# Batch 0 loaded in runs of nine rows, cast on chip and transposed in bf16; other loads released later; instruction order from a priority table that counts tile switches

## The chip, the cores and the metric

The kernel runs on one core of a Trainium2 chip. A core has five engines that each work through a queue of their own in order: TensorE (PE, matrix products and transposes into the eight PSUM banks), VectorE (DVE), ScalarE (ACT), GpSimd (POOL) and SyncE (SP, which here only issues transfers). Sixteen DMA engines move data for all queues. Engines and transfers wait for each other on semaphores. The metric is the device time of one execution in microseconds.

## The reference

Linear attention with exponential features, then a gated unit with a causal convolution of five taps. Eight batches, eight heads, 576 rows, head width 64, 128 features, model width 512.

```python
def phi(x):                                   # x: q or k
    proj = np.einsum('bhsd,df->bhsf', x, w_phi)
    proj = proj - np.max(np.abs(proj), axis=-1, keepdims=True)
    return np.concatenate([np.exp(proj), np.exp(-proj)], axis=-1)
q_p, k_p = (phi(q), phi(k))
kv = np.einsum('bhsf,bhsd->bhfd', k_p, v)
z = np.sum(k_p, axis=2)
num = np.einsum('bhsf,bhfd->bhsd', q_p, kv)
den = np.einsum('bhsf,bhf->bhs', q_p, z)[..., None] + 1e-06
attn = num / den                              # heads side by side give x: (batch, 576, 512)
gate_pre[:, s] = sum over k of conv_w[k] * x[:, s - 4 + k]      # zero before the first row
out = ((1 / (1 + np.exp(-gate_pre))) * (x @ w_val)) @ w_out
```

## The kernel before

A planner in the kernel's source builds the program. `build` makes a list of operations; each has a name, the engine or engines that may run it, an estimated duration, what it reads and writes, a priority (`prio`, smaller is earlier) and for some an earliest time (`rel`). `Plan.schedule` plays them through a list scheduler: at each moment a free engine takes, of the operations whose inputs are there, whose PSUM banks are free and whose `rel` has passed, the one with the smallest priority. The planner's times are used for nothing but the order; `Plan.emit` writes the instructions to the engines' queues in that order, with the semaphore waits that the data needs. So `rel` is not a wait on the chip: a later `rel` only puts a transfer further back in its queue.

A batch goes through these operations (in brackets the number per batch):

- loads. q and k of batches 1 to 7: `cast` [4] is a GpSimd transfer from f32 to bf16 into a DRAM buffer R, `tr` [4] a transposing SyncE transfer of R into KT or QT. v comes by `v` [2] and `vt` [1, four transfers]. Two halves, g = 0 and 1, hold four heads each.
- batch 0 has another way, since nothing can be prefetched for it: `xf` [4, SyncE, lines 417 to 422] loads q and k in f32 as 18 blocks of 128x128 each, 512 contiguous bytes at a time, in the order k g=0, q g=0, k g=1, q g=1, into XF, which lies in the space of batch 1's QTIL (shown as QTIL in the profile); `T0` [12, three transposes each, line 428] turns them on TensorE in f32, and `T0c` [12] copies PSUM to KT or QT.
- features of k: `K`, `Kt` project on TensorE; `Kmax` takes the row maxima on VectorE; `Kexp` the exponentials of both signs on ScalarE, without subtracting the maxima; `MN` and `EK` make exp of the maxima; `VT`, `VTt` (GpSimd, line 537 and 547) scale v by it.
- features of q: `QA`, `Qmax`, `MQ`, `MQc` find the maxima and turn them; `QF` projects and subtracts them, `Qexp` exponentiates.
- `KV` [2] and its copy `KVc`; `NUM` [4] and `NUMt` with `RCP` and `NRM` (division); `XT`, `XTt`, `XTc` transpose the result.
- `GATE` [4] is the convolution as products with diagonal matrices DG (built once by GpSimd, line 397), `TANH` the gate, `VAL` [4] the value product, `GV` their product; `OUT` [4, in odd batches 5], `OUTc`, `store`.

Operations of different products use different shapes of TensorE's array: 128*128 (KV, NUM, XT, MQ, OUT), 64*128 (K, QA, QF, VAL), 128*64 (GATE, NUMt, XTt), and 64*32 or 128*32 for small rests.

The priority of an operation is `period * batch + offset`, with one offset per name and one step (`Kd`, `QAd` and so on) per index; `limit` says how many PSUM tiles of a kind may live at once. Weights (`WVa`, `WO`) are loaded by GpSimd with casts at priorities -195 and -194, w_phi and conv_w by ScalarE's queue.

Of the kernel before, what the change touches and what calls it, by code (L numbers as in the profile page):

```python
# [8 lines left out]
AF = mybir.ActivationFunctionType  # L9
# [21 lines left out]
PE_L = 0.19  # L31
# [8 lines left out]
    off=dict(  # L40
        cast=-28.24, v=-6.0, DG=8.07, K=0.0, Kd=4.34, QA=1.0, QAd=4.0, EK=2.83, VT=1.85, MQ=15.13,
        QF=19.55, QFd=3.59, KV=21.26, KVd=3.55, NUM=27.88, NUMd=3.0, XT=1.6, GATE=41.98, GATEd=3.0,
        OUT=55.38, OUTd=1.94, store=0.5,
# [21 lines left out]
class Plan:  # L65
# [4 lines left out]
    def __init__(self):  # L70
        self.ops, self.tok = [], {}
# [6 lines left out]
    def op(self, name, eng, occ, fn, prio, r=(), w=(), ps=None, new=False, vis=None, dma=None, key=None,  # L78
           rel=0.0):
# [8 lines left out]
        o.name, o.fn, o.prio, o.dma, o.key, o.ps, o.new, o.rel = name, fn, prio, dma, key, ps, new, rel  # L88
        hard, soft = set(), set()
# [19 lines left out]
        o.deps = [(x, True) for x in hard] + [(x, False) for x in soft]  # L109
# [7 lines left out]
    def _from(self, x, hard, e):  # L117

        if x.eng == e:
            return x.t2 if hard and e != "PE" else x.t1  # L120
        return x.t2 + WAKE

    def schedule(self, limit):
# [8 lines left out]
        for o in self.ops:  # L132
            if not o.need:
                for e in o.opts:
                    ready[e].append(o)
# [6 lines left out]
        order = []  # L142
        left = len(self.ops)
        while left:
# [4 lines left out]

            while pend and pend[0][0] <= t + 1e-9:  # L150
                s, _, o = heapq.heappop(pend)
                dma_now = self._share(queues, dma_now, s, times)
                queues.setdefault(o.eng, []).append([o, o.dma])
            dma_now = self._share(queues, dma_now, t, times)
# [4 lines left out]
            while again:  # L159
                again = False  # L160
                for e in self.ENG:
# [25 lines left out]
                    for f in o.opts:  # L187
                        ready[f].remove(o)
                    o.eng, o.t0 = e, t
                    o.t1, o.t2 = t + o.occ[e], t + o.vis[e]  # L190
                    if o.dma is not None:
                        o.t2 = 1e9
                        heapq.heappush(pend, (o.t1 + 0.6, o.seq, o))
                        heapq.heappush(times, o.t1 + 0.6)
# [3 lines left out]
                    if ps is not None:  # L198
# [8 lines left out]
                        else:  # L207
# [3 lines left out]
                            if not ps.left:  # L211
# [4 lines left out]
                                heapq.heappush(times, o.t2 + WAKE)  # L216
                    for x in (o.t1, o.t2, o.t2 + WAKE):
                        if x < 1e8:
                            heapq.heappush(times, x)
                    order.append(o)  # L220
                    for c in o.outs:
                        c.need -= 1
                        if not c.need:
                            for f in c.opts:
                                ready[f].append(c)
        self.order = order
        for s, _, o in pend:
            queues.setdefault(o.eng, []).append([o, o.dma])
        self._share(queues, dma_now, 1e7, times)
# [3 lines left out]
    def _share(queues, now, t, times):  # L233
        import heapq
        while now < t:
# [9 lines left out]
            for y in act:  # L245
                y[0][1] -= d / len(act)
                if y[0][1] < 1e-9:
                    o = y.pop(0)[0]
                    o.t2 = now + 1.4
                    heapq.heappush(times, o.t2)  # L250
                    heapq.heappush(times, o.t2 + WAKE)
# [12 lines left out]
    def emit(self, tc, nc):  # L264
# [29 lines left out]
        with tc.tile_critical(name="main"):  # L294
            for o in self.order:
# [10 lines left out]
                for k, n in need.items():  # L306
                    E.wait_ge(sems[k], n)
                    for kk, nn in snap[(k, n)].items():
                        if kn.get(kk, 0) < nn:
                            kn[kk] = nn  # L310
                out = o.fn(E, None if o.ps is None else o.ps.at)
# [20 lines left out]
def build(pl, cfg, nc=None, m=None):  # L332
# [13 lines left out]
    def const(name, eng, occ, fn, prio, r=(), w=(), **kw):  # L346
# [13 lines left out]
          -150, r=["ident_f"], w=["ident_bf"])  # L360
# [32 lines left out]
    const("cwt", "PE", 1.2, cwt, -90, r=["cwb", "idp"], ps=cwps, new=True)  # L393
    const("CWT", "DVE", 0.15, lambda E, b: [E.tensor_copy(m.CWT[:, :], m.PS[:, b, 0:48])], -89, w=["CWT"], ps=cwps)
    pl.fresh("DG")
    for h in range(H):
# [5 lines left out]
        m.WV[0:D, :, :], m.w_val.rearrange("(h c) j -> c h j", c=D))], -195, w=["WVa"], dma=3.1, key=("WVa",))  # L402
# [547 lines left out]
```

## Time and profile before

| | us |
|---|---|
| median of 2 runs | 258.6 (258.54 to 258.65) |
| the profiled execution | 258.6 |
| its span, first to last instruction | 256.8 |
| TensorE busy | 206.9 |
| VectorE busy | 181.5 |
| ScalarE busy | 174.6 |
| GpSimd busy | 119.1 |

The page of the profile gives busy time per engine, the chain of waits that ended last, groups of instructions by line, and the DMA queues. Views of the trace add the instructions in order of time, waits, and busy time by stretch. L428 is line 428 of the kernel's source. A row of the time line merges neighbouring instructions of one group; its last brackets give the idle time of the engine before them and what ended it.

### The profile page before, as it was taken

How to read it: one execution, taken by the hardware profiler on the slowest of the kernel's cores; microseconds unless marked ns; L12 is line 12 of the kernel's file. 1: busy time of each engine (PE TensorE's matmuls, PEld its weight loads, DVE VectorE, ACT ScalarE, POOL GpSimd, SP SyncE). 2: the span in 40 equal slices, each digit the busy share in tenths (PEclk: the TensorE clock that was granted, in tenths of full speed). 3: DMA queues.
4: the chain of work that ended last, by engine and by line, in shares of the span. 5: the costliest groups of instructions: out<-in, count | busy, mean ns of one | idle time of the engine just before them, and what ended most of it. 6: DMA issues, size and time to landing. Idle time of an engine off the chain costs nothing.

```text
span 256.8 us, 8459 instructions
## 1 busy us (share of the span) xinstructions
PE 206.9 (81%) x3693; PEld 144.7 (56%) x3708; DVE 181.5 (71%) x277; ACT 174.6 (68%) x240; POOL 119.1 (46%) x203
## 2 busy tenths in 40 slices
PE   0260838487968999899899999998998999999960
PEld 0250626466646577657675766576666766775520
DVE  0163583696679977997899778997898797376450
ACT  5031468963498899788898978878998895662300
POOL 8434396477418575716863572167316904200000
PEclk9999977897999999999999999999999999999997
DMA  6999999999535999789999993960170013103041
GB/s 185 200 242 213 315 235 198 240 214 240 131 67 67 214 232 304 150 96 193 214 227 214 250 211 97 218 187 19 21 211 31 3 52 136 24 0 151 17 162 43
DMA packets 58495, 39.95 MB, mean 156 GB/s; under 512 B 39381, under 2 KB 53333, under 8 KB 57946
## 3 DMA queue, kind: packets, MB, share of 16 engines
q1 hardware_dynamic: 56336, 30.03, 49.3%
q0 software_dynamic: 1952, 9.31, 20.2%
q8 instruction: 29, 0.48, 0.8%
q10 hardware_dynamic: 170, 0.08, 0.1%
q14 instruction: 8, 0.07, 0.1%
HBM read 30.48 MB, written 17.69 MB: 188 GB/s over the span
## 4 chain that ended last, share of the span: by engine, by line
PE 59%; DVE 16%; ACT 11%; DMA 9%; issue 2%; SPq 0%; DVEq 0%
PE PS L787 11%; PE PS L813 10%; DMA QTIL<-in_k_dram 9%; PE PS L776 9%; PE PS L665 7%; ACT QTIL L625 6%; DVE MQb L586 5%; PE PS L701 4%; ACT KTIL L500 3%; DVE MK L495 3%; PE PS L612 3%; PE PS L720 2%; PE PS L490 2%; PE PS L618 2%; DVE GV L792 2%
## 5 line engine op out<-in xcount | busy, mean ns | idle before, releaser
L537 POOL TENSOR_TENSOR VT<-VN,EK 128x512 bf16<-128x512 f32 x64 | 65.7, 1045 | 18.8 <-ACT EK L528 18.7
L625 ACT ACTIVATE QTIL<-PS 128x1024 bf16<-128x1024 f32 x64 | 61.9, 1036 | 12.6 <-PE PS L618 12.6
L500 ACT ACTIVATE KTIL<-PS 128x1024 bf16<-128x1024 f32 x64 | 62.5, 1032 | 6.4 <-PE PS L490 4.3
L586 DVE TENSOR_REDUCE MQb<-PS 128x8 bf16<-128x1024 f32 (+1 forms) x40 | 44.1, 1113 | 3.1 <-PE PS L574 2.6
L495 DVE TENSOR_REDUCE MK<-PS 128x8 f32<-128x1024 f32 x32 | 39.0, 1219 | 4.6 <-PE PS L490 2.7
L792 DVE SCALAR_TENSOR_TENSOR GV<-GS,PS 128x576 bf16<-128x576 bf16 x32 | 24.1, 753 | 18.8 <-PE PS L787 14.6
L787 PE MATMUL PS<-XT,WV 64*128 64x288 bf16 x512 | 37.1, 283 | 0.1
L782 ACT ACTIVATE GS<-PS 128x576 bf16<-128x576 f32 x32 | 21.1, 661 | 19.6 <-PE PS L776 19.3
L525 POOL TENSOR_SCALAR MK<-MK 128x16 f32<-128x16 f32 (+1 forms) x24 | 5.9, 244 | 58.6 <-DVE MK L495 55.3
L776 PE MATMUL PS<-XT,DG 128*64 128x288 bf16 x384 | 30.1, 292 | 2.4 <-ACT QTIL L625 1.4
L813 PE MATMUL PS<-WO,GV 128*128 128x512 bf16 x113 | 28.3, 379 | 2.9 <-DVE GV L792 1.1
L787 PEld LDWEIGHTS PS<-XT,WV 64*128 64x128 bf16 x512 | 22.9, 94 | 8.8 <-issue 1.6
L665 PE MATMUL PS<-VT,KTIL 128*128 128x65 bf16 x512 | 22.6, 202 | 2.2 <-ACT QTIL L625 1.3
L776 PEld LDWEIGHTS PS<-XT,DG 128*64 128x64 bf16 x384 | 19.2, 110 | 8.4 <-ACT QTIL L625 1.7
L665 PEld LDWEIGHTS PS<-VT,KTIL 128*128 128x128 bf16 x512 | 20.2, 103 | 5.1 <-issue 4.3
L715 DVE TENSOR_TENSOR XN<-PS,RC 128x512 bf16<-128x512 f32 x32 | 22.0, 690 | 0.9
L701 PE MATMUL PS<-KVSB,QTIL 128*128 128x65 bf16 x512 | 20.6, 193 | 1.3 <-DVE MQb L586 0.9
L547 POOL TENSOR_TENSOR VTt<-VNt,EK 128x512 bf16<-128x512 f32 x16 | 16.6, 1042 | 9.3 <-ACT EK L528 9.2
L428 PE MATMUL PS<-ident_f,QTIL 128*128 128x128 f32 x36 | 8.7, 425 | 14.2 <-DMA QTIL<-in_k_dram 12.7
L701 PEld LDWEIGHTS PS<-KVSB,QTIL 128*128 128x128 bf16 x512 | 17.4, 97 | 4.3 <-DVE MQb L586 1.4
L679 DVE CAST KVSB<-PS 128x520 bf16<-128x520 f32 x16 | 11.2, 699 | 11.5 <-PE PS L670 11.3
L813 PEld LDWEIGHTS PS<-WO,GV 128*128 128x128 bf16 x128 | 11.1, 98 | 12.0 <-DVE GV L792 1.2
(74 smaller groups left out, 285.2 us busy)
## 6 DMA issues: line engine op xcount, KB each, us to landing
VN<-in_v_dram SPq DMA_DIRECT2D x16, 512.0 KB, 6.2
out_dram<-OS SPq DMA_DIRECT2D x32, 256.0 KB, 3.4
R<-in_k_dram POOLq DMA_DIRECT2D x14, 288.0 KB, 6.1
R<-in_q_dram POOLq DMA_DIRECT2D x14, 288.0 KB, 6.3
QTIL<-in_k_dram SPq DMA_DIRECT2D x2, 576.0 KB, 14.6
QTIL<-in_q_dram SPq DMA_DIRECT2D x2, 576.0 KB, 19.6
VNt<-in_v_dram SPq DMA_DIRECT2D x32, 32.0 KB, 4.4
out_dram<-OS SPq DMA_DIRECT2D x16, 64.0 KB, 2.0
```

The lines of the kernel that those rows point to most:

```text
L495: pl.op("Kmax", "DVE", dve(1024), lambda E, at, u=u: [E.tensor_reduce(MK[:, 0, 8 * u:8 * u + 8].rearrange("p (t x) -> p t x", t=2), m.PS[: ...
L500: pl.op("Kexp", "ACT", act(1024), lambda E, at, u=u, g=g: [E.activation(KTIL[:, g, u, :, :, :], m.PS[:, at:at + 2, :].rearrange("p t (x f) ...
L537: pl.op("VT", "POOL", pool(512), lambda E, at, u=u, hh=hh, a=a, g=g, EK=EK: [E.tensor_tensor(m.VT[s][:, g, u, :, :, 0:D], m.VN[s][:, 4 * h ...
L586: pl.op("Qmax", "DVE", dve(256 * nx), lambda E, at, u=u, nx=nx: [E.tensor_reduce(MQb[:, :].rearrange("p (t s) -> p t s", t=2)[:, :, 4 * u: ...
L625: pl.op("Qexp", "ACT", act(1024), lambda E, at, u=u, g=g: [E.activation(m.QTIL[s][:, g, u, :, :, :], m.PS[:, at:at + 2, :].rearrange("p t ...
L665: res.append(E.matmul(m.PS[:, at + sg, x * E1:(x + 1) * E1], m.KTIL[s][:, sg, 2 * g + a, par, x, :], m.VT[s][:, sg, 2 * g + a, par, x, :], ...
L701: return [E.matmul(m.PS[:, at + g, x * E1:(x + 1) * E1], m.QTIL[s][:, sg, 2 * j + g, par, x, :], m.KVSB[s][:, g, sg, x, :], start=(sg == 0 ...
L715: pl.op("NRM", "DVE", dve(512), lambda E, at, view=view, RC=RC, XN=XN, par=par: [E.tensor_tensor(XN[:, :, par, :].rearrange("p (g x) d -> ...
L776: return [E.matmul(m.PS[ROWS[hh], at + p, 0:HALF], m.DG[:, 2 * jt + hh, 3 * p + dl, :], XT[:, 2 * jt + hh, dl:dl + HALF], start=(dl == 0), ...
L787: return [E.matmul(m.PS[:, at + p, 0:HALF], m.WV[ROWS[p], h, P * jt:P * jt + P], XT[ROWS[p], h, PAD:PAD + HALF], start=(h == 0), stop=(h = ...
L792: pl.op("GV", "DVE", dve(576), lambda E, at, jt=jt, GS=GS: [E.scalar_tensor_tensor(out=m.GV[jt][:, s, :, :], in0=GS[:, :, :], scalar=1.0, ...
L813: return [E.matmul(m.PS[:, at, :], m.GV[jt][:, s, p, P * j:P * j + P], m.WO[:, jt, :], start=(jt == 0), stop=(jt == 3)) for jt in range(4)]
```

## The change

It has five parts.

1. Batch 0's `xf` reads nine rows of 128 as one run of 4608 bytes per partition. A new operation `XB` [12] casts three blocks from f32 to bf16 into a buffer in the space of batch 1's KTIL, on VectorE, ScalarE or GpSimd; `T0` transposes bf16; `T0c` writes each ninth column. Odd batches' `Kexp` wait for all XB and T0, as `Qexp` did for T0.
2. `rel` of other loads: batch 1's casts, v, the weights and later batches' casts get entries in tables `rel1` (batches 0 and 1, absolute) and `rel` (later batches, added to `period * batch`). Batch 1's casts have the entries -30.91, 14.39, -96.98 and -10.45, negative ones meaning 0; `v` of batches 0 and 1 has 18.34 and 20.69, WVa 26.92, WO 45.71.
3. `weigh` replaces each priority by one from tables for all batches (`fine`) or for batch 0, batch 1 and the last (`first`, `second`, `last`), one entry per name and index, between about -440 and 172. The tables have about 700 entries, left out below but for some lines.
4. The planner counts a change of TensorE's tile shape as 0.095 us, prefers an operation of the present shape by a `bonus` of 4.41, has new durations, releases what waits for a transfer only when it has landed, and limits other numbers of PSUM tiles. `period` is 24.15.
5. Reuse of a buffer on one engine becomes a dependence of the kind that is waited for; RC has four buffers in place of three.

```diff
 CFG = dict(
-    period=19.0,
+    period=24.15,
+    bonus=4.41,
     limit=dict(
-        K=1, QA=1, QF=3, KV=1, NUM=2, XT=2, MQ=1, GATE=1, VAL=1, OUT=2, T0=3,
+        T0=2, K=2, QA=1, MQ=2, QF=4, KV=3, NUM=3, XT=2, GATE=2, VAL=4, OUT=4,
     ),
...
+    fine=dict(
+        v=(24.2, 51.69,), vt=(84.37,), cast=(-13.35, 37.02, -0.83, 14.17,), tr=(-75.29, -368.41, 15.75,
+        -126.26,), K=(-14.91, -0.84, 15.06, 22.29,), Kmax=(-290.23, 59.46, 70.03, 124.55, -17.49,), Kexp=(63.16,
...
+    first=dict(
...
+        WVb=(-41.19,), WO=(11.86,), xf=(65.3, -63.63, -269.39, 65.64,), XB=(89.84, 39.94, 102.51, -55.53, 28.87,
...
+    rel=dict(
+        v=(2.53, 1.56,), vt=(-7.25,), cast=(-16.04, -20.18, -7.87, -25.82,),
+    ),
+    rel1=dict(
+        WVa=(26.92,), WO=(45.71,), v=(18.34, 20.69,), vt=(17.22,), cast=(-30.91, 14.39, -96.98, -10.45,),
     ),
...
-        o.deps = [(x, True) for x in hard] + [(x, False) for x in soft]
+        o.deps = [(x, True) for x in hard] + [(x, True) for x in soft]
...
+    def weigh(self, cfg):
+        T, last = cfg["period"], max(o.b for o in self.ops)
+        for o in self.ops:
+            for part, on in (("fine", True), ("first", o.b == 0), ("second", o.b == 1), ("last", o.b == last)):
+                x = cfg.get(part, {}).get(o.name)
+                if on and x is not None and o.idx < len(x):
+                    o.prio = T * o.b + x[o.idx]
+            x = cfg.get("rel" if o.b > 1 else "rel1", {}).get(o.name)
+            if x is not None:
+                o.rel = max(0.0, T * o.b * (o.b > 1) + x[o.idx])
...
+                        now = (o.prio - bonus if o.mode is not None and o.mode == pe_mode else o.prio, o.seq)
+                        if best is not None and now >= best_now:
                             continue
...
+                    if e == "PE":
+                        sw = PE_SWITCH if pe_mode is not None and o.mode != pe_mode else 0.0
+                        pe_mode = o.mode
...
-                    src = (m.k, m.q)[xi][0].rearrange("h s d -> (h s d)").rearrange("(c p x) -> p c x", p=P, x=P)
+                    src = (m.k, m.q)[xi][0].rearrange("h s d -> (h s d)").rearrange("(g p cx) -> g p cx", g=2, cx=9 * P)
                     pl.fresh(("XF", xi, g))
                     pl.op("xf", "SP", 0.6, lambda E, b_, xi=xi, g=g, src=src: [E.dma_start(
-                        m.XF[:, 18 * xi + 9 * g:18 * xi + 9 * g + 9, :], src[:, 9 * g:9 * g + 9, :])],
-                        -300 + 2 * g + xi, w=[("XF", xi, g)], dma=1.95, key=("XF", xi, g))
+                        m.XF[:, 18 * xi + 9 * g:18 * xi + 9 * g + 9, :].rearrange("p c x -> p (c x)"), src[g])],
+                        -300 + 2 * g + xi, w=[("XF", xi, g)], dma=1.5, key=("XF", xi, g))
...
+                        pl.op("XB", ("DVE", "ACT", "POOL"), {"DVE": dve(384, True), "ACT": act(384), "POOL": 0.8},
+                              lambda E, at, c=c: [cp(E, m.XB[:, c:c + 3, :], m.XF[:, c:c + 3, :])],
+                              pr, r=[("XF", xi, g)], w=[("XB", c)])
+                        pl.op("T0", "PE", 0.2, lambda E, at, c=c: [E.transpose(
+                            m.PS[:, at, :].bitcast(BF16)[:, P * y:P * y + P], m.XB[:, c + y, :], m.ident_bf[:, :])
+                            for y in range(3)], pr, r=[("XB", c), "ident_bf"], w=[], ps=ps, new=True, mode="F")
+                        dst = 1152 * g
                         pl.op("T0c", ("DVE", "ACT"), {"DVE": dve(384), "ACT": act(384)},
+                              lambda E, at, X=X, dst=dst, j=j: [cp(
+                                  E, m.T[X][0][:, dst:dst + 1152].rearrange("p (i c) -> p c i", c=9)[:, 3 * j:3 * j + 3, :],
+                                  m.PS[:, at, :].bitcast(BF16)[:, 0:384].rearrange("p (c i) -> p c i", c=3))],
+                              pr, w=[(X, 0, g)], ps=ps)
...
-        if x.name == "T0":
+        if x.name in ("T0", "XB"):
             pl.tok["xfdone"].w.append(x)
```

## Rows read from the trace of the kernel before

**Rows 1.** By stretch: us, busy us (count) per engine, PEclk, DMA share, GB/s
```profile
0.00:26.00 26.00, 7.10 (x74) 5.58 (x74) 7.47 (x19) 6.75 (x6) 12.90 (x30) 1.00 0.97 212
...
26.00:60.00 34.00, 22.40 (x383) 17.40 (x384) 22.75 (x33) 24.56 (x34) 21.99 (x35) 0.84 1.14 236
...
80.00:230.00 150.00, 142.85 (x2708) 99.24 (x2714) 124.88 (x187) 125.59 (x176) 74.92 (x123) 1.00 0.66 144
...
230.00:250.00 20.00, 17.40 (x211) 9.85 (x208) 11.94 (x21) 4.23 (x7) 0.00 (x0) 1.00 0.27 99
```

**Rows 2.** Page, parts 1 and 4: busy per engine; last-ending chain by engine
```profile
PE 206.9 (81%) x3693; PEld 144.7 (56%) x3708; DVE 181.5 (71%) x277; ACT 174.6 (68%) x240; POOL 119.1 (46%) x203
...
PE 59%; DVE 16%; ACT 11%; DMA 9%; issue 2%; SPq 0%; DVEq 0%
```

**Rows 3.** Time line, start: start us, us, engine, line, operation, count [idle before]
```profile
14.16 0.60 PE L490 MATMUL PS<-W,KT 64*128 64x128 bf16 x8 [0.29 <-DVE KT L471]
...
26.35 2.18 PE L428 MATMUL PS<-ident_f,QTIL 128*128 128x128 f32 x9 [6.59 <-DMA QTIL<-in_k_dram]
...
32.70 4.05 POOL L537 TENSOR_TENSOR VT<-VN,EK 128x512 bf16<-128x512 f32 x4
...
37.40 0.29 PE L592 MATMUL PS<-ident_bf,MQb 128*128 128x128 bf16 x1 [2.46 <-DVE MQb L586]
...
49.29 0.93 PE L665 MATMUL PS<-VT,KTIL 128*128 128x65 bf16 x14 [1.30 <-ACT QTIL L625]
...
52.44 1.68 PE L701 MATMUL PS<-KVSB,QTIL 128*128 128x65 bf16 x48 [0.25 <-DVE KVSB L679]
```

**Rows 4.** Time line: KV of batches 0 and 7; last cast; batch 7's K
```profile
40.68 1.06 PE L665 MATMUL PS<-VT,KTIL 128*128 128x65 bf16 x16
...
147.58 0.54 POOL L441 DMA_DIRECT2D R<-in_q_dram  x1
...
193.90 0.39 PE L490 MATMUL PS<-W,KT 64*128 64x128 bf16 x8
...
215.67 0.66 PE L665 MATMUL PS<-VT,KTIL 128*128 128x65 bf16 x16
```

**Rows 5.** Time line of TensorE: first and last row counted, prices between
```profile
93.52 1.16 PE L787 MATMUL PS<-XT,WV 64*128 64x288 bf16 x16
...
94.52 0.39 PE L490 MATMUL PS<-W,KT 64*128 64x128 bf16 x8
...
95.69 1.16 PE L787 MATMUL PS<-XT,WV 64*128 64x288 bf16 x16
...
96.79 0.66 PE L665 MATMUL PS<-VT,KTIL 128*128 128x65 bf16 x16
...
228.70 0.62 PE L720 MATMUL PS<-ident_bf,XN 128*128 128x128 bf16 x8
```

**Rows 6.** DMA queues (packets, MB, share); issues (count, KB, us to landing)
```profile
q1 hardware_dynamic: 56336, 30.03, 49.3%
...
q0 software_dynamic: 1952, 9.31, 20.2%
...
R<-in_k_dram POOLq DMA_DIRECT2D x14, 288.0 KB, 6.1
...
KT<-R SPq DMA_TRANSPOSE x14, 5.5
```

**Rows 7.** Groups by line: busy us, mean ns of one, idle before
```profile
L537 POOL TENSOR_TENSOR VT<-VN,EK 128x512 bf16<-128x512 f32 x64 | 65.7, 1045 | 18.8 <-ACT EK L528 18.7
...
L397 POOL TENSOR_TENSOR DG<-I,CWT 128x384 bf16<-128x384 bf16 x8 | 6.4, 826 | 5.3 <-DVE CWT L394 5.3
...
L378 DVE CAST cwb<-cw 5x512 bf16<-5x512 f32 x1 | 0.4, 414 | 1.1 <-DMA cw<-in_moe_conv_w_dram 1.1
...
L471 DVE CAST KT<-PS 128x384 bf16<-128x384 f32 x5 | 2.6, 544 | 6.7 <-PE PS L428 6.6
```

**Rows 8.** By stretch, as the first group: the granted clock fell
```profile
36.00:42.00 6.00, 4.28 (x54) 3.09 (x55) 2.70 (x4) 3.84 (x7) 3.71 (x5) 0.50 1.13 306
```

More of the change, by code (lines that the diff above doesn't have):

```diff
@@ new lines @@
+    second=dict(
+        v=(40.44, 28.51,), vt=(27.96,), cast=(23.57, 57.22, -17.6, -23.17,), tr=(26.1, 27.48, 90.23, 93.93,),
+        K=(111.65, -3.03, -8.73, 28.89,), Kmax=(-193.96, -26.15, 52.35, 40.92, 13.5,), Kexp=(24.94, -9.91,
+        78.31, 38.75, 57.7, 13.17, -45.9, -26.59, -2.37, 121.42,), MN=(49.47, 93.47, 68.19,), EK=(-89, 13.35,
+        25.02,), VT=(-141.28, -6.07, 37.62, 87.24, 63.36, 32.85, 99.98, 8.89,), VT1=(-251.15, -184.04, 66.09,
+        -76.63,), Kt=(-123.51,), VTt=(-85.09, -111.26,), VTt1=(8.2, -121.3,), QA=(-43.93, 62.57, 31.99, 66.56,
+        -0.8,), Qmax=(-62.38, -23.47, -284.75, 44.06, 76.21,), MQ=(-7.08,), MQc=(65.08,), QF=(59.37, -118.11,
+        73.54, -291.73, 46.87,), Qexp=(-323.62, 58.9, 2.24, -247.94, -150.63, -245.14, 88.11, 150.09, -156.45,
+        35.28,), KV=(15.2, -161.51,), KVc=(-275.02, 1.95,), NUM=(43.93, 48.62, -23.08, 47.59,), RCP=(74.67,
+        -22.86, 95.06, -26.26, 92.85,), NRM=(96.75, 101.65, -0.72, -59.55, -59.48,), XT=(21.52, -116.87,),
+        XTc=(29.22, 47.53, -72.51,), NUMt=(39.47,), XTt=(-55.08,), GATE=(-61.84, -83.13, -33.12, 8.5,),
+        TANH=(-126.15, -3.02, -98.9, -58.71,), VAL=(-204.48, -178.47, 54.38, 12.11,), GV=(-35.77, 140.24, -4.28,
+        9.4,), OUT=(-2.86, 114.61, 87.26, 7.53, 97.4,), OUTc=(-54.65, 21.77, 45.52, 73.45, -23.79,),
+        store=(37.14, 65.94, -14.51, 2.1, 26.12,),
+    ),
@@ new lines @@
+    last=dict(
+        v=(-24.49, 46.58,), vt=(90.74,), cast=(87.65, -4.14, 8.43, -21.92,), tr=(-8.64, -80.95, -5.15, 49.71,),
+        K=(-74.63, -0.22, 51.58, 34.63,), Kmax=(28.59, -59.55, 26.12, 64.06, 62.22,), Kexp=(96.47, -88.6, -9.32,
+        39.15, 17.09, 133.15, -24.24, -124.82, -169.42, 22.3,), MN=(65.13, -72.09, -129.79,), EK=(-15.84, 30.04,
+        -12.95,), VT=(-293.34, 35.47, 33.35, -1.49, -16.59, 49.03, 51.42, -5.56,), VT1=(-18.61, -177.51, 3.26,
+        -249.55,), Kt=(-18.89,), VTt=(66.53, -15.46,), VTt1=(72.62, 66.75,), QA=(11.57, -302.19, 41.84, 29.36,
+        -88.87,), Qmax=(-20.97, 85.06, -272.67, 112.38, 3.18,), MQ=(79.77,), MQc=(45.37,), QF=(66.77, -216.05,
+        -128.06, 24.96, 88.2,), Qexp=(-17.76, -37.99, -182.84, 32.84, 48.45, 20.3, 59.36, -78.56, 55.03,
+        24.22,), KV=(2.99, 69.5,), KVc=(-213.37, 0.89,), NUM=(-244.09, -4.19, 20.32, -395.47,), RCP=(2.89,
+        -63.1, 59.65, 7.73, 110.39,), NRM=(105.64, -31.27, -121.24, -287.88, -0.35,), XT=(64, 25.84,), XTc=(24,
+        -227.02, -307.05,), NUMt=(41.99,), XTt=(-22.29,), GATE=(-105.74, -55.15, 25.2, 13.25,), TANH=(30.13,
+        71.69, -270.96, -86.04,), VAL=(21.67, 34.12, 36.1, 53.01,), GV=(-21.26, 14.5, -27, 4.51,), OUT=(38.35,
+        -148.99, 59.91, 27.95, -299.84,), OUTc=(22.03, -27.67, -47.05, -42.72, -36.29,), store=(-275.16, 50.47,
+        -91.16, 68.38, 8.16,),
+    ),
@@ L141, in schedule, with arm, landed @@
         times = sorted({0.0} | {o.rel for o in self.ops})
-        order = []
+        order, pe_mode = [], None
         left = len(self.ops)
+        def arm(o):
+            o.rdy = {}
+            for e in o.opts:
+                o.rdy[e] = max([o.rel] + [self._from(x, h, e) for x, h in o.deps])
+                ready[e].append(o)
+        def landed(done):
+            for x in done:
+                heapq.heappush(times, x.t2 + WAKE)
+                for c in x.outs:
+                    c.need -= 1
+                    if not c.need:
+                        arm(c)
+        for o in self.ops:
+            if not o.need:
+                arm(o)
         while left:
@@ L215, in schedule @@
                                     bank_free[k] = o.t2 + WAKE
[L216 to L219, printed above, removed]
                     order.append(o)
+                    heapq.heappush(times, o.t1)
+                    if o.dma is not None:
+                        o.t2 = 1e9
+                        heapq.heappush(pend, (o.t1 + 0.6, o.seq, o))
+                        heapq.heappush(times, o.t1 + 0.6)
+                        continue
+                    heapq.heappush(times, o.t2)
+                    heapq.heappush(times, o.t2 + WAKE)
                     for c in o.outs:
@@ L246, in _share @@
                 y[0][1] -= d / len(act)
+            for y in act:
                 if y[0][1] < 1e-9:
@@ L249, in _share @@
                     o.t2 = now + 1.4
-                    heapq.heappush(times, o.t2)
-                    heapq.heappush(times, o.t2 + WAKE)
+                    done.append(o)
         return t
@@ L651, in kv @@
     def kv(b):
+        pl.b = b
         s = b % 2
@@ L906 @@
     m.XN = [t(f"XN{s}", [P, H, 2, D]) for s in range(3)]
-    m.RC = [t(f"RC{s}", [P, 2, 4], FP32) for s in range(3)]
+    m.RC = [t(f"RC{s}", [P, 2, 4], FP32) for s in range(4)]
     m.XNt, m.RCt = [t(f"XNt{s}", [P, 4, D]) for s in two], [t(f"RCt{s}", [P, 4], FP32) for s in two]
```

194 lines of the change are left out of this document (114 added, 80 removed).

## Prediction, made before the change was run

> **What bounds the kernel now.** I read the stages first [rows 1]: per stretch, the busy time of each engine and the DMA share. In the first 26 us TensorE works 7.10 us, VectorE 7.47, ScalarE 6.75, while the sixteen DMA engines are full (0.97): the start is bound by transfers. From 80 to 230 us TensorE is busy 142.85 of 150 us, with VectorE (124.88) and ScalarE (125.59) not far behind; the DMA share is 0.66. At the end TensorE runs almost alone (17.40 of 20 us against 11.94 and 4.23). The chain of waits that ended last agrees: TensorE 59%, VectorE 16%, ScalarE 11%, DMA 9% [rows 2].
>
> The time line of the start shows where this hurts [rows 3]. Third in line, `xf` of k for g=1 lets TensorE begin its transposes at 26.35 us, after 6.59 us of waiting. VT of batch 0 begins on GpSimd at 32.70, the second KV (heads of g=1) on TensorE at 49.29, the first NUM at 52.44.
>
> The steady pace: batch 0's first KV is at 40.68, batch 7's at 215.67, so 175.0/7 = 25.0 us a batch [rows 4]. In the list of TensorE's instructions from 93.52 to 228.70 us (first and last row in [rows 5]), 5.4 batches, I counted 140 places where neighbouring rows change the shape of the array's tile (128*128, 64*128, 128*64, and so on), 26 a batch, and 5.1 us of idle time, 0.9 a batch. One change costs 0.10 us: VAL takes 1.00 us up to the K behind it (same shape, 93.52 to 94.52) and 1.10 up to a KV (other shape, 95.69 to 96.79) [rows 5]. So a batch is 26 x 0.10 = 2.6 of changes, 0.9 idle and, by subtraction, 21.5 of work that no order of instructions removes.
>
> **The change part by part.** The sum is made against the profiled execution: span 256.8 and 1.8 around it, 258.6, which is also the median of the runs.
>
> *The start.* Before the third `xf` landed, the 25.2 us of DMA time (0.97 x 26, [rows 1]) held four `xf`, eight casts (batches 1 and 2) and WV and WO. The software queue took 20.2% of 256.8 = 51.9 us for 9.31 MB [rows 6], 5.6 us a MB: 1.64 us for a cast (0.295 MB), 2.9 for a weight (0.52 MB). Eight casts 13.1 and two weights 5.8 leave 6.3 for the `xf`, 1.6 each. The tables release three casts of batch 1 at 0 and put batch 2's and both weights later, so the four `xf` share with 4.9 us of casts: 6.3 + 4.9 = 11.2, plus 1 before the first issue and something to landing: all four by about 14 us. Batch 0's inputs gain 12 to 16 us. The longer runs may make `xf` cheaper too; I count nothing for it.
>
> What is late next is `v`, which stands on SyncE behind transposes that wait for the casts. Up to its landing the engines move 11.2, one more cast 1.6, three transposes and `v` (0.885 and 1.18 MB; the hardware queue took 49.3% of 256.8 = 126.6 us for 30.03 MB [rows 6], 4.2 a MB: 3.7 and 5.0), 21.5 in all, so it lands at 23 to 24. Then GpSimd has eight VT and two VTt at 1.045 [rows 7] and their small parts, some 12 us: the second KV at 36 to 37, the first NUM near 40. Against 52.44 that is 12 us, which I take. The ends: 7, if `v` comes at 26 and the DG instructions (6.4 us, [rows 7]) fall between the VT; 16, if the whole gain of the inputs passes through.
>
> *Cast, bf16 transposes, strided copies.* Twelve XB are new. VectorE's nearest casts are 0.414 for 512 columns and 0.544 for 384 out of PSUM [rows 7]; 12 x 0.35 to 0.54 = 4.2 to 6.5 us, spread over three engines of which VectorE and ScalarE are idle for over 70% of the start [rows 1], and one XB, about 0.4, on the path of each run. The transposes pay that back: nine in f32 take 2.18 [rows 3], eight in bf16 0.62 [rows 5], some 1.5 less a run. T0c writes every ninth column; at twice its price it adds 6.5 us over two engines, hidden the same way. If that cover is gone, 2 us. Sum 0, ends -1 and +2. The new wait of odd batches' Kexp for all XB costs nothing: XB must be done before batch 0's Kmax can be, and batch 1's Kexp comes behind that. Waits for reuse on the same engine fall on instructions some places back in its queue: 0. The fourth RC can save no more than part of the 0.9 idle; it is in the next term.
>
> *Order and tile switches.* Nothing is removed from the steady work; the table can save only switches and idle time. Its entries spread over hundreds of us while the bonus is 4.41, so the bonus decides only between near neighbours; the larger limits (VAL 1 to 4, NUM 2 to 3, KV 1 to 3) let equals stand together. I take a third fewer switches (26 to 17.5, 0.85 us) and 0.3 of the idle time: 1.15 a batch, over seven batches 8.0. Ends: 0, and 2.2 a batch or 15, since VectorE's 181.5 us [rows 2] less some 8 at the start is 21.7 a batch and ScalarE's 174.6 less some 7 is 21.0: below 22.8 neither could wait much at all. At the end TensorE's work is the same; 0.
>
> [...]
>
> The sum: 258.6 - 12.0 - 8.0 + 0 = 238.6 us.
>
> **The rivals.**
> - *Only the start gains*, the order stays as costly: VectorE's 83% and ScalarE's 84% from 80 to 230 us [rows 1], with a hand-over at each step, speak for it. 258.6 - 12 = 246.6.
> - *Both gain to their ends*; VectorE is the next bound. 258.6 - 15 - 15 = 228.6.
> - *The start's gain is eaten by what lands next*: `v` and batch 1's transposes are late, gain 4, pace half as good, 4: 250.6. For it: the share is 1.14 from 26 to 60 us too [rows 1]. Against: half of the casts and the weights are gone from there.
> [...]
> - *Slower*: casts are issued by GpSimd in order behind VT, which wait for EK (18.7 us in all [rows 7]). Before, batch 7's last cast was issued at 147.58, 46 us ahead of its first K at 193.90 [rows 4]; the tables release casts at -26 to -8 us and K at -15 to 22, a lead of some 15, while cast and transpose take 6.1 + 5.5 to land [rows 6]. Each us of lateness beyond that is paid in every batch: over six batches the gain of 20 and 5.2 more are gone at 4.2 us a batch; 264 from there. Against it: the waits must first use up what is left of the lead.
> - *No difference*: an order that fits the planner's times and not the real ones trades switches for idle time: 256.
>
> **How the numbers follow.** Forecast 0.44 (231 to 245), clock 0.08, only the start 0.17, both to their ends 0.12, start eaten 0.06, no difference 0.08, slower 0.05. The range 227 to 250 leaves out the last two, half of the eaten start and a third of the best case: 0.20. Faster by over 2% (below 253.4; about what a measurement of this kernel can tell from no change): 0.44 + 0.08 + 0.17 + 0.12 + 0.06 = 0.87; within it 0.08; slower 0.05.
>
> **What would show each step right or wrong.** Right: the last T0 group before 16 us; VT of batch 0 near 24 and the first NUM near 40; KV to KV 23.9 us a batch; some 17 or 18 changes of shape a batch; the DMA share of the first 15 us still near 1. Wrong: T0 groups waiting beyond 20 us (the sharing of the DMA engines), VT starting at 30 or later (`v`), 25 us a batch with fewer switches but more idle time (the order), a granted clock of 0.50 through 15 to 40 us, K waiting for a transpose in batches 2 to 7 (casts too late).

## The result and the profile after

The kernel after takes 250.9 us (median; 250.5 to 251.3) against 258.6: a ratio of 0.970, 95% interval 0.963 to 0.977. The forecast was 238.6 in a range of 227 to 250. The sign was right, and the time lies just beyond the range. Some executions of the kernels with the new order are several us longer than others of the same kernel, so the times and ratios below are of the runs within 1.5% of a kernel's fastest, and a kernel with only one such run gets no ratio.

The first GATE instruction of a batch on TensorE splits the gain. Time line of TensorE, first GATE of batch 0 and of batch 7; the kernel before (line 776), then the one after (line 898):

```profile
61.99 1.32 PE L776 MATMUL PS<-XT,DG 128*64 128x288 bf16 x12
...
235.58 0.93 PE L776 MATMUL PS<-XT,DG 128*64 128x288 bf16 x12
```

```profile
62.00 1.72 PE L898 MATMUL PS<-XT,DG 128*64 128x288 bf16 x24 [0.25 <-DVE XT L845]
...
228.45 3.14 PE L898 MATMUL PS<-XT,DG 128*64 128x288 bf16 x48
```

| part | before | after | measured | forecast |
|---|---|---|---|---|
| to GATE of batch 0 | 62.0 | 62.0 | 0 | -12.0 |
| seven batches, to GATE of batch 7 | 173.6 | 166.45 | -7.1 | -8.0 |
| from there to the end of the span | 21.2 | 20.05 | -1.2 | 0 |
| span | 256.8 | 248.5 | -8.3 | -20.0 |

By this marker the order of the steady batches gave nearly what was forecast, and the start gave nothing at all. The split depends on the marker, because the new order puts the work around it in another sequence. The forecast of the start was made for the first NUM. Batch 0's stands at 52.44 in [rows 3]; here are batch 7's before, then batches 0 and 7 after:

```profile
224.03 0.66 PE L701 MATMUL PS<-KVSB,QTIL 128*128 128x65 bf16 x16
```

```profile
56.04 0.66 PE L822 MATMUL PS<-KVSB,QTIL 128*128 128x65 bf16 x16
...
222.09 2.11 PE L822 MATMUL PS<-KVSB,QTIL 128*128 128x65 bf16 x64
```

By it the start is 3.6 us longer, the seven batches are 5.5 shorter and the rest 6.4 shorter. The 8.3 us of the span depend on no marker, nor does a comparison of kernels that have one order. The same stretches as [rows 1], of the kernel after:

```profile
0.00:26.00 26.00, 6.83 (x91) 4.90 (x91) 15.96 (x25) 14.59 (x14) 13.13 (x31) 1.00 0.75 195
26.00:60.00 34.00, 23.89 (x423) 16.74 (x424) 24.77 (x33) 31.21 (x42) 19.43 (x33) 1.00 0.73 142
80.00:230.00 150.00, 145.07 (x2754) 102.68 (x2754) 121.39 (x190) 125.47 (x177) 78.50 (x127) 0.99 0.75 166
230.00:250.00 20.00, 10.33 (x122) 5.97 (x118) 6.47 (x9) 2.02 (x4) 0.00 (x0) 0.85 0.23 79
```

In the first 26 us the DMA share fell from 0.97 to 0.75: the start is no longer bound by transfers. VectorE went from 7.47 to 15.96 us and ScalarE from 6.75 to 14.59, and TensorE still did only 6.83. So something on VectorE and ScalarE took the place of the transfers. The page's busy time and its chain by engine, which answer to [rows 2], show it on the chain too: TensorE's share fell from 59% to 50%.

```profile
PE 203.6 (82%) x3708; PEld 143.5 (58%) x3708; DVE 183.3 (74%) x276; ACT 184.9 (74%) x250; POOL 120.5 (48%) x206
...
PE 50%; ACT 15%; DVE 13%; DMA 11%; SPq 4%; POOL 2%; issue 2%; ACTq 0%; DVEq 0%
```

Which instructions these are stands in the groups by line, forms kept apart, of 0 to 40 us (count | busy us, mean ns of one | idle before):

```profile
L587 DVE COPY QT<-PS 128x384 bf16<-128x384 bf16 x4 | 7.0, 1949 | 0.0
L585 ACT ACTIVATE KT<-PS 128x384 bf16<-128x384 bf16 x3 | 5.4, 1961 | 0.8 <-PE PS L542 0.8
L587 DVE COPY KT<-PS 128x384 bf16<-128x384 bf16 x3 | 5.4, 1910 | 0.0
...
L585 ACT ACTIVATE QT<-PS 128x384 bf16<-128x384 bf16 x2 | 3.7, 1863 | 1.7 <-PE PS L542 1.7
```

These are the T0c copies, PSUM to KT and QT, which now write every ninth bf16 of a row. Before, a copy of the same 384 columns took 0.544 us [rows 7]; now one takes 1.86 to 1.96 on either engine. The twelve are 22 us of work, and they do not hide. In the chain of waits that ended last (start us, us, what), nine of them stand between 10.9 and 32.8 us:

```profile
2.05 8.48 DMA wtmp<-in_w_phi_dram
10.55 0.23 DVE W L475
10.90 3.44 DVE KT L587 x2
...
16.27 3.43 DVE QT L587 x2
...
20.48 1.88 ACT QT L585
...
23.48 3.54 ACT KT L585 x2
...
29.37 3.45 DVE QT L587 x2
```

That is 3.44 + 3.43 + 1.88 + 3.54 + 3.45 = 15.7 us. The last `xf`, issued at 2.33, landed 12.2 us later, at 14.6, about as forecast; but K of batch 0 waits for the copies, Kmax and EK for K, and VT for EK. Time line of GpSimd; VT of batch 0 answers to the row at 32.70 in [rows 3]:

```profile
33.71 0.24 POOL L641 TENSOR_SCALAR MK<-MK 128x16 f32<-128x16 f32 x1 [8.55 <-DVE MK L612]
...
37.81 3.05 POOL L653 TENSOR_TENSOR VT<-VN,EK 128x512 bf16<-128x512 f32 x3
```

GpSimd sat idle for 8.55 us until the maxima of K were there. VT, forecast at 24, began at 37.81 and did not wait for `v`, and the first NUM came at 56.04 (before 52.44).

The steady batches have a flaw of their own. From first NUM to first NUM most take 23.1 to 24.0 us, but batch 6's came 28.8 us after batch 5's. There GpSimd, ScalarE and TensorE wait one behind the other, for the second of two `v` that SyncE issued from 168.58 on, which landed at 178.02; the waits are in brackets:

```profile
178.10 2.04 POOL L653 TENSOR_TENSOR VT<-VN,EK 128x512 bf16<-128x512 f32 x2 [6.90 <-DMA VN<-in_v_dram]
...
180.37 0.21 ACT L644 ACTIVATE EK<-MK 128x8 f32<-128x8 f32 x1 [3.68 <-POOL MK L641]
...
183.81 0.40 PE L691 MATMUL PS<-W,QT 64*128 64x128 bf16 x8 [2.95 <-DVE MK L612]
```

### The profile page after: what moved, and what is told of

It reads as the page before. It is cut to its first block, busy times and chain, and to the rows that moved or that the text cites. A ratio compares the mean times of both kernels' runs of the same rounds, so it can differ in the third digit from the quotient of the medians.

```text
span 248.5 us, 8457 instructions
## 1 busy us (share of the span) xinstructions
PE 203.6 (82%) x3708; PEld 143.5 (58%) x3708; DVE 183.3 (74%) x276; ACT 184.9 (74%) x250; POOL 120.5 (48%) x206
## 4 chain that ended last, share of the span: by engine, by line
PE 50%; ACT 15%; DVE 13%; DMA 11%; SPq 4%; POOL 2%; issue 2%; ACTq 0%; DVEq 0%
PE PS L909 10%; PE PS L936 8%; DMA VN<-in_v_dram 7%; PE PS L898 7%; PE PS L785 5%; ACT KTIL L617 5%; ACT QTIL L744 5%; PE PS L822 4%; DVE MQb L704 4%; DMA wtmp<-in_w_phi_dram 3%; DVE QT L587 3%; DVE MK L612 3%; PE PS L731 3%; PE PS L691 2%; ACT GS L904 2%; PE PS L607 2%
## 5 line engine op out<-in xcount | busy, mean ns | idle before, releaser
L909 PE MATMUL PS<-XT,WV 64*128 64x288 bf16 x512 | 35.7, 284 | 1.1 <-ACT OS L585 0.4
L936 PE MATMUL PS<-WO,GV 128*128 128x512 bf16 x128 | 32.1, 380 | 0.2 <-DVE XT L845 0.2
L898 PE MATMUL PS<-XT,DG 128*64 128x288 bf16 x384 | 28.6, 297 | 0.8 <-ACT GS L904 0.5
L909 PEld LDWEIGHTS PS<-XT,WV 64*128 64x128 bf16 x512 | 24.3, 94 | 7.8 <-issue 0.9
L898 PEld LDWEIGHTS PS<-XT,DG 128*64 128x64 bf16 x384 | 20.5, 112 | 8.6 <-DVE XT L879 1.3
L691 PE MATMUL PS<-W,QT 64*128 64x128 bf16 x256 | 14.6, 239 | 10.7 <-ACT QT L585 4.0
L607 PE MATMUL PS<-W,KT 64*128 64x128 bf16 x256 | 13.9, 240 | 10.0 <-DVE KT L587 7.0
L785 PE MATMUL PS<-VT,KTIL 128*128 128x65 bf16 x512 | 20.7, 196 | 0.2
L585 ACT ACTIVATE OS<-PS 128x512 f32<-128x512 f32 x23 | 13.9, 609 | 6.2 <-PE PS L936 6.2
L691 PEld LDWEIGHTS PS<-W,QT 64*128 64x128 bf16 x256 | 8.8, 103 | 15.5 <-issue 8.3
```

The costliest lines, as they stand in the source:

```text
L691: res.append(E.matmul(m.PS[:, at + par, P * x:P * x + P], QT[ROWS[par], 4 * hh + x, P * j:P * j + P], m.W2[ROWS[par], :], start=True, stop ...
L785: res.append(E.matmul(m.PS[:, at + sg, x * E1:(x + 1) * E1], m.KTIL[s][:, sg, 2 * g + a, par, x, :], m.VT[s][:, sg, 2 * g + a, par, x, :], ...
L898: return [E.matmul(m.PS[ROWS[hh], at + p, 0:HALF], m.DG[:, 2 * jt + hh, 3 * p + dl, :], XT[:, 2 * jt + hh, dl:dl + HALF], start=(dl == 0), ...
L909: return [E.matmul(m.PS[:, at + p, 0:HALF], m.WV[ROWS[p], h, P * jt:P * jt + P], XT[ROWS[p], h, PAD:PAD + HALF], start=(h == 0), stop=(h = ...
L936: return [E.matmul(m.PS[:, at, :], m.GV[jt][:, s, p, P * j:P * j + P], m.WO[:, jt, :], start=(jt == 0), stop=(jt == 3)) for jt in range(4)]
```

## The experiments

Theory S: the price of the strided copies took the start's gain. Its rivals: `w_phi`, whose transfer is the first 8.48 us of that chain, and the casts that were added. For the batches two questions are open: whether the order's gain is one of tile switches, and what the late `v` costs. "Short rows" below always means the kernel of the first experiment.

**Short rows.** `xf` again in 512-byte rows, so T0c writes its 384 columns next to each other; the order of all work is untouched.

```diff
-    .rearrange("(g p cx) -> g p cx", g=2, cx=9 * P)
+    .rearrange("(c p x) -> p c x", p=P, x=P)
...
-    dst = 1152 * g
+    dst = 1152 * g + 384 * j
...
-    E, m.T[X][0][:, dst:dst + 1152].rearrange("p (i c) -> p c i", c=9)[:, 3 * j:3 * j + 3, :],
-    m.PS[:, at, :].bitcast(BF16)[:, 0:384].rearrange("p (c i) -> p c i", c=3))],
+    E, m.T[X][0][:, dst:dst + 384], m.PS[:, at, :].bitcast(BF16)[:, 0:384])],
```

> The changed kernel in the same order of instructions, but xf reads 512 bytes at a time again and T0c writes contiguous columns; the cast and the bf16 transposes stay. Theory S (the strided T0c, 1.85 us each, hold up the start): T0c falls to about 0.55, some 11 us of the 15.7 that these copies take of the chain of waits go, the first NUM moves from 56.0 to about 45, and the kernel takes about 240. Theory D (v and the transposes of batch 1 bind the start): T0c falls the same, but the first NUM moves by less than 4 us and the kernel stays above 247.

Measured: 238.7 us, ratio 0.923 (0.918 to 0.928). The copies by line and form, 0 to 40 us, and the first GATE of batches 0 and 7:

```profile
L584 ACT ACTIVATE KT<-PS 128x384 bf16<-128x384 bf16 x3 | 1.4, 489 | 0.8 <-PE PS L542 0.8
L586 DVE COPY QT<-PS 128x384 bf16<-128x384 bf16 x4 | 1.2, 348 | 0.0
```

```profile
49.78 1.72 PE L897 MATMUL PS<-XT,DG 128*64 128x288 bf16 x24 [0.25 <-DVE XT L844]
...
216.61 3.14 PE L897 MATMUL PS<-XT,DG 128*64 128x288 bf16 x48
```

By the first GATE the start is 12.2 us shorter than before (forecast 12.0) and the batches take 166.8 (6.8 less); by the first NUM, at 43.81, the start is 8.6 shorter. Against the kernel after, which has the same order, either marker gives 12.2. The copies' prices give nearly that: the nine of the chain, six on VectorE and three on ScalarE, cost 6 x 0.35 + 3 x 0.49 = 3.6 in place of 15.7, which is 12.1 less. That the two agree so closely is partly chance, since the chain of the short rows is another one. Three copies (1.27 us) are left on it, 14.5 less, and it begins with the third `xf`, which in short rows lands at 13.64 and in runs of nine landed at 9.86:

```profile
2.12 11.53 DMA QTIL<-in_k_dram
```

In the kernel after, what came first on the chain ended at 10.53, so the transfers of the short rows take 3.1 us of the 14.5 back. Theory S holds.

**Three in a row.** Runs of nine rows as in the change, but each copy writes three neighbours, then skips to the next nine (the same elements land in the same places, in another sequence).

```diff
-    .rearrange("p (i c) -> p c i", c=9)[:, 3 * j:3 * j + 3, :],
-    ....rearrange("p (c i) -> p c i", c=3))],
+    .rearrange("p (i c) -> p i c", c=9)[:, :, 3 * j:3 * j + 3],
+    ....rearrange("p (c i) -> p i c", c=3))],
```

> The changed kernel, runs of nine rows kept, but T0c goes through its columns in another sequence: three neighbouring bf16 are written in a row, and PSUM is read with a stride of 256 bytes instead. If the price of T0c lies in writing single elements 18 bytes apart, a third of the jumps is left: about 0.8 us each and 243 us for the kernel. If it lies in the pattern as such or in what PSUM gives, T0c stays at 1.8 or grows, and the time at 250 or above.

Measured: 243.9 us, ratio 0.943 (0.937 to 0.948), first GATE at 54.04. By line and form, 0 to 40 us:

```profile
L587 DVE COPY QT<-PS 128x384 bf16<-128x384 bf16 x4 | 2.6, 705 | 0.0
L585 ACT ACTIVATE KT<-PS 128x384 bf16<-128x384 bf16 x3 | 2.0, 738 | 0.8 <-PE PS L542 0.8
```

How scattered the writes are sets the price here, not the run of nine itself and not the strided read of PSUM, which this kernel has and the kernel after had not: 384 single elements 18 bytes apart 1.9 us, 128 triples 0.71, one block 0.35 on VectorE. And 8.0 us of the start come back of the 12.2. The price follows the number of separate pieces that a copy writes, 384, 128 or one; what in a scattered write takes the time is not shown.

**w_phi first.** The kernel after, with `w_phi`'s two loads issued first, on SyncE.

```diff
-    E.dma_start(m.wtmp[0:D, :], ...), E.dma_start(m.wtmp[D:P, :], ...)
+    nc.sync.dma_start(m.wtmp[0:D, :], ...), nc.sync.dma_start(m.wtmp[D:P, :], ...)
...
+    pl.order.sort(key=lambda o: o.name != "w_phi")
```

> The changed kernel, but w_phi's two loads are issued first of all on SyncE instead of second on ScalarE. Theory W (VectorE stands behind the cast of w_phi, which lands at 10.5 us, and the copies behind it come late): the cast is done by 4 us, the first copy by VectorE starts near 6 instead of 10.81, the first NUM comes 4 to 5 us earlier and the kernel takes about 246. Theory S alone: the copies are the bound wherever they start, the gain is below 2 us.

Measured: 245.5 us, ratio 0.950 (0.945 to 0.955), the time of theory W. In the profiled execution (251.4 us) `w_phi` landed by 3.7 in place of 10.53, but its cast W came at 6.63 in place of 10.55, behind a cast that waited for the first `xf`; the first GATE stands at 59.0 and the first NUM at 53.03, 3.0 us earlier and not 4 to 5. The 8.48 us on the chain are worth these 3.0 at the start, a quarter of the loss: a second, smaller cause. In short rows `w_phi` is off the chain, so its gain is had within theirs. Where the rest of the 5.4 us between 250.9 and 245.5 came from is open.

**w_phi first with short rows.** The same edit on short rows.

> Short rows, same order of work, and w_phi's two loads issued first, on SyncE. With short rows the cast W2 came at 8.45 us and the first K at 9.38. Theory (W2 is on the path of the start there too): W2 near 6.6 as in the run with w_phi first on long rows, K near 8, start and time 1 to 1.5 us less: 237.3. Rival (the first transposes are what the first K waits for, and v lands no sooner): within 0.5 us of 238.7.

Measured: 236.2 us in the quickest of four runs, 241.4, 243.9 and 382.5 in the others; short rows had 237.1 to 239.7. In the profiled execution (241.4 us) W came at 7.01 and not 8.45, but the first K only at 8.82 in place of 9.38, and the second `xf` to be used, q's, was waited for until 12.65; the first NUM came at 46.04, not 43.81. No gain is seen there; whether there is one is open.

**Transposes in f32.** Short rows; XB is cut to one element each, and TensorE transposes the rows in f32.

```diff
-    cp(E, m.XB[:, c:c + 3, :], m.XF[:, c:c + 3, :])
+    cp(E, m.XB[:, c:c + 1, 0:1], m.XF[:, c:c + 1, 0:1])
...
-    m.PS[:, at, :].bitcast(BF16)[:, P * y:P * y + P], m.XB[:, c + y, :], m.ident_bf[:, :])
+    m.PS[:, at, P * y:P * y + P], m.XF[:, c + y, :], m.ident_f[:, :])
```

> Short rows, same order of work; the cast on chip is cut to one element each (so it does no work) and PE transposes the rows in f32 as the kernel before did. This prices the part of the change that the prediction summed to 0 (casts cost 4 to 6 us over three engines, bf16 transposes give back 1.5 us a run of nine). Theory P (they cancel): within 1 us of 238.7. Rival (the casts stand on the path of the start): 236 to 237, since each run then saves one cast of 0.35 to 0.7 us ahead of its transposes. [...]

Measured: 238.4 us, ratio 0.922 (0.920 to 0.923) against 0.923 for short rows: the same. Its 36 transposes took 9.2 us where the bf16 ones of the kernel after took 4.9; the casts that buy this took 6.8 us in short rows (VectorE 3.1, ScalarE 2.1, GpSimd 1.6). Cast and bf16 transposes cancel, as the prediction's sum had them.

**The priorities of before.** Short rows and the cast on chip in the new planner, with the priorities, releases and limits of the kernel before, no bonus and no tables.

```diff
-    period=24.15, bonus=4.41, limit=dict(T0=2, K=2, ...), off=dict(T0=2.07, ...), fine=..., first=..., ...
+    period=19.0, bonus=0.0, limit=dict(K=1, QA=1, ...), off=dict(cast=-28.24, ...)
...
-    pl.weigh(CFG)
```

> The short rows, cast and bf16 transposes of the first experiment, in the changed planner, but with the priorities, releases and PSUM limits of the kernel before, without bonus and without the tables. Theory O (the tables earn the pace): 25.0 us from KV to KV and some 26 changes of tile shape a batch as before, about 256 to 258 us. Rival (the planner's new durations and dependences earn it): near 24 us a batch and about 250.

Measured: 261.6 us, ratio 1.013 (1.007 to 1.018). In the profiled execution (264.4 us) the first GATE stands at 56.79, and then a batch takes 26.3 us. From its first GATE to the end TensorE changes its tile's shape 193 times (short rows 144, the kernel before 192). That is theory O, with batches slower than the 25.0 us it said. Without the tables, limits, releases and bonus the change would have gained nothing: together they are worth 23 us, and 49 changes fewer at 0.10 us [rows 5] are only 4.9 of those.

**No bonus.** Short rows with all tables, but no bonus for keeping a tile shape; the planner makes its order anew.

```diff
-    bonus=4.41,
+    bonus=0.0,
```

> Short rows, with the tables, limits and releases of the change but the bonus for staying with a tile shape set to 0, so the planner makes another order. Theory of the prediction (the bonus saves the switches, 0.10 us each): the changes of tile shape go from about 21 a batch back towards 26, and each of the seven batches costs 0.5 us more: 242 to 243. Rival (the tables' entries, which were fitted with the bonus, carry the gain through what they do to the waits, and the switches are small change): either the shape changes stay near 21 and the time near 238.7, or batches grow by more than 1 us through waits that the switches do not explain: 246 or more.

Measured: 260.1 us, ratio 1.006 (1.003 to 1.009). Changes of shape in the whole run: 203 against 174. So the forecast's theory falls for this step, and the rival holds: 29 changes are 2.9 us, and 21 are lost. The tables' entries are worth their gain only together with the bonus, and most of it is not in switches. That it is in waits follows only by subtraction; which waits stays open.

**v earlier, in batches 2 to 7.** Short rows; on SyncE `v` of a batch ahead of the transpose of k that it stood behind.

```diff
+    for b_ in range(2, 8):      # on SyncE, order otherwise kept
+        ...move v(b_, 0), v(b_, 1) ahead of the first transpose of k of batch b_
```

> Short rows, same order of work, but in batches 2 to 7 v stands on SyncE ahead of the transpose of k that it stood behind. That transpose waits for a cast, which GpSimd issues behind VT, and VT waits for v: a loop. Theory L (the loop costs the pace): in the run with short rows undisturbed batches took 23.0 us and those in which VT waited 3.4 to 6.6 us for v took 24 to 29; the wait of VT for VN (17.0 us in all) goes below 3, seven batches take 23.0 to 23.3 each in place of 23.8, and the time is 238.7 less 4 to 6: 233 to 235. Rival (the late v only shows another lateness, that of the casts behind VT, and the transposes come late all the same): VT no longer waits for v, but K or QA waits for the transposes, and the time stays at 237 to 239.

Measured: 248.2 us, ratio 0.960 (0.955 to 0.964), 9.5 us worse than short rows. Waits by who waits for whom (us in total, times, longest), short rows and then this run:

```profile
POOL VT L652 <- DMA VN<-in_v_dram: 17.0, 5, 6.6
```

```profile
PEld PS L606 <- DMA KT<-R: 11.0, 3, 5.3
```

VT's wait for `v` is gone, and K now waits for the transposes behind it: those into KT took a median of 7.0 us from issue to landing, in place of 5.3. A wait on GpSimd, which in short rows made two batches take 26.2 and 27.1 us in place of 23 to 24, was traded for one on TensorE. The expectation's rival holds, and worse than it said: neither `v` nor the transposes have any lead left.

**The casts together.** Short rows; in batches 3 to 7 GpSimd issues the four casts of a batch in a row, where the first stood.

> Short rows, same order of work, but in batches 3 to 7 the four casts of a batch stand together on GpSimd where the first of them stood, so the last one (k, heads of g=1) is issued some 13 us and the one of k g=0 some 6 us earlier. In the run with v moved ahead of the transposes, K waited up to 5.0 us for a transpose, so neither v nor the transposes had any lead left. Theory C (the lead of the casts is what is used up): the transposes no longer wait for casts, v behind them comes earlier too, VT's wait for v (17.0 us with short rows) goes below 5 us, K does not wait for transposes, seven batches take about 23.1 each: 232 to 235. Rival (the DMA engines or SyncE's queue, not the casts' place, set when transposes and v land): four casts of 0.295 MB in a row collide with transposes and stores, VT goes on waiting for v, 237 to 241.

Measured: 236.2 us in the quickest of four runs, 243.8 to 246.8 in the others; short rows had 237.1 to 239.7, so whether it gains is open. In the profiled execution (243.8 us) VT's wait for `v` fell to 6.9 us (theory C: below 5), and K waits for no transpose. On the chain of waits the four issues now stand between VT and VT in four batches, 1.9 us each time; whether they cost what the earlier casts give is not shown. One piece of the chain:

```profile
108.86 3.05 POOL VT L652 x3
...
112.24 1.92 POOL R L556 x4
114.16 1.07 POOL VT L652
```

**Casts together and v earlier.**

> As the run with the casts together, and v of batches 2 to 7 ahead of the transposes of k on SyncE as well (that alone took 247 to 258). Theory C: with the casts earlier the transposes can afford v ahead of them, so the loss of that run is gone and the time is 232 to 235. Rival (SyncE's queue is what makes the transposes late): K goes on waiting 3 to 5 us for transposes in some batches, 242 to 252.

Measured: 243.2 us in the quickest of four runs, 247.7 to 250.5 in the others. In the profiled execution (248.3 us) K waits up to 6.0 us for transposes, as the rival has it. So the casts' place alone does not make them late; that SyncE's queue and the transfers in it do the rest is likely, but not shown.

**v of batch 0 earlier, alone and with the rest.** Short rows; `v` and `vt` of batch 0 ahead of batch 1's transposes. In the second kernel also `v` of batches 2 to 7 earlier, and `w_phi` first.

> Short rows as in the run of 238.7 us, same order of work, but v and vt of batch 0 stand on SyncE ahead of batch 1's transposes, so they no longer wait for the casts that feed those. Theory V (what is late next is v, as the prediction put it): in the run with short rows VT of batch 0 began at 26.1 us, though EK was there at 15.6; v then lands near 16, VT begins near 17 and the first NUM (43.8) comes 3 to 5 us earlier: 234 to 236. [...] Rival (v takes DMA time from the last xf and from batch 1's casts): the first NUM is later, 240.

> All together on the kernel with short rows: v of batch 0 ahead of batch 1's transposes, v of batches 2 to 7 ahead of the transposes of k, and w_phi's two loads issued first, on SyncE. If theories V and L both hold, 238.7 - 3 - 5 = 231, and w_phi, which the cast W2 awaited at 8.45 us there, gives at most 1 more: 229 to 232. If only L holds: 233 to 235. If neither: 237 to 239.

Measured: the first took 234.1 us in the quickest of four runs, the number of theory V, and 239.8 to 244.7 in the others, which decides nothing about the time. In its profiled execution (244.7 us) `v` landed at 16.8 and 18.4, about as theory V has it, but VT of batch 0 began at 28.13, against 26.11 with short rows: it came behind VTt, which waited for EK, and the first NUM came at 46.51. With short rows VT had waited 0.24 us for `v`, and VTt 0.48 for `vt`: `v` and EK arrive close together there, and in this execution the earlier `v` saved nothing. The second took 246.9 in the quickest run and 250.9 to 260.7 in the others: the loss of `v` ahead of the transposes again. Nothing run here beats short rows by a measured margin.

## Why the prediction was right or wrong

- **What bounds the kernel, and the transfers of the start**: right in kind. The last `xf` landed at 14.6 us (about 14). With short rows VT began at 26.1 (24) and the first NUM came at 43.8 (40), so the start gave 8.6 us at the forecast's own marker, where 12.0 were taken, and 12.2 at the first GATE. That short rows take the 238.6 of the forecast is in part luck: by the first NUM they save 8.6 us at the start, 5.2 in the seven batches and 6.4 behind them, where 12.0, 8.0 and 0 were forecast. `v` as what is late next holds there by 0.24 us only, 0.72 with `vt`. In the kernel after, VT at 30 or later came true as a sign of being wrong, but not for `v`, which had landed at 34.4: VT began at 37.81 because of the copies.
- **Cast, bf16 transposes, strided copies**: here is the step that failed, in the sentence "T0c writes every ninth column; at twice its price it adds 6.5 us over two engines, hidden the same way". The term was the copies, put at 0 with ends of -1 and +2; it measured 12.2 at the start. Both halves of the sentence were wrong. The price is 3.5 times that of [rows 7], and 4 to 5.5 times that of the same copies in one block: the twelve took 21.5 us in place of 4.6. And the cover was not there: VectorE and ScalarE idle for 70% of the start [rows 1] is an average of a stretch that waited for transfers. Once these are early, each copy stands between a transpose and the K or QA that reads it, and nine of the twelve stood on the chain. That no row of before showed a strided write should have given the term an upper end by the count of scattered elements, not by a guess of twice. The rest of the part, cast against bf16 transposes, came out at 0. Its 1.5 us a run set f32 rows of the start (nine in 2.18 at 26.35 us [rows 3]) against bf16 rows of the end (eight in 0.62 at 228.70 [rows 5]); both in the start, 9.2 and 4.9 us for all 36 transposes, it is 1.1 a run.
- **Order and tile switches**: by the first GATE -7.1 for -8.0. From there to the end, which is 8.3 us shorter, TensorE changes shape 144 times (192 before): 48 x 0.10 = 4.8 us, where 6.0 were forecast. (From 80 to 230 us it is 129 times, 160 before: some 20.5 a batch and not 17.5.) Its idle time there fell from 10.1 to 8.0 us, 2.1, as forecast. The other 1.4 I can't place. So the terms were the right ones, but the reason behind them was not: the bonus, which the prediction thought of as a decision between near neighbours, makes 21 us of difference, and only 2.9 of these are switches. Batches that no late `v` disturbs take 23.1 to 24.0, about the forecast's 23.9; one stall of 5 us is in the seven. The releases and the new kind of dependence (parts 2 and 5) were not tried by themselves.
- **The ends**: by the first GATE 1.2 us came at the end, by the first NUM 6.4; forecast 0.
- **The clock**: the sign that the prediction names, a granted clock of 0.50 through 15 to 40 us, did not come: in the kernel after and with short rows the granted clock was 1.00 in each stretch from 0 to 60 us. The kernel before had 0.50 from 36 to 42 [rows 8] and 0.84 from 50 to 60. TensorE's products took longer in the start all the same. In the kernel after K took 0.61 us at 39.37, 0.63 at 48.00 and 0.40 at 163.68, and 16 KV took 1.09 at 50.95 and 0.66 at 53.49: the longer times last until about 52. With short rows they last until about 41 (16 KV in 1.08 at 38.42, in 0.66 at 41.27). In the kernel before K took 0.60 at 14.16 [rows 3] and 0.40 at 34.54, and then 16 KV took 1.06 at 40.68 [rows 4], 1.04 at 49.29 and 1.06 at 59.69. What makes a product longer at a granted clock of 1.00 is not shown. The forecast's sum counts 0 for the clock, and no run shows that term by itself; what the runs show in its place are these longer times of TensorE, and short rows took 238.7 us with them.
- **The rivals**: "the start's gain is eaten by what lands next" gave 250.6, which is nearly the number measured, but not its mechanism: it wanted full DMA engines from 26 to 60 us, and their share fell from 1.14 to 0.73. The mechanism of "slower" was there: batch 7's last cast was issued at 184.62, 6.7 us ahead of its first K at 191.31, where before it had 46 [rows 4]:

```profile
184.62 0.58 POOL L557 DMA_DIRECT2D R<-in_k_dram  x1
```

```profile
191.31 0.39 PE L607 MATMUL PS<-W,KT 64*128 64x128 bf16 x8
```

From 60 us on SyncE's transposes waited five times for a cast, 12.9 us in all; before, once, for 3.3. `v` stands behind these transposes. Its late landing cost about 5 us in one batch, and it came to no more.

## What to carry to other kernels

A longer contiguous run for a DMA can move its stride to somewhere else, here to the copies out of PSUM: find the instruction that takes it over, and price that by its scattered elements, not by its count of columns (384 columns took 1.9 us here one by one, 0.71 in threes, 0.35 in one block on VectorE). An idle share over a stretch that waits for something need not cover anything once that something is early (nine of the twelve copies, 15.7 us, came to stand on the chain); ask which instructions stand in a row between the new arrival and the work that needs it. In an order whose lead is used up, moving one transfer ahead can move the wait instead of ending it: `v` ahead of the transposes took it from GpSimd (17.0 us for `v`) to TensorE (11.0 us for the transposes), and the kernel took 9.5 us more.

## What was not expected of the hardware

- 384 bf16 out of PSUM cost the same on VectorE and ScalarE when each lands 18 bytes from the last (1.91 to 1.95 and 1.86 to 1.96 us), though in one block VectorE takes 0.35 and ScalarE 0.49.
- A load of 32 KB twice (`w_phi`), issued on ScalarE's queue from 1.50 on, landed at 10.5 us beside the four `xf` of SyncE's queue; issued ahead of them on SyncE's queue it landed by 3.7.
- The order is touchy: short rows take 238.7 us, 248.2 with `v` of batches 2 to 7 moved ahead, and 260.1 in the order that the planner makes without the bonus.
